# Lightning attention and a cosine-gated MLP on one core: a list scheduler's order, an enforced order of transfers, tiles of 4,2,4,4,4,4,2 blocks and other PSUM banks at both ends

## The chip, the cores and the metric

One core of one Trainium2 chip runs the kernel. The metric is the device time of one launch in microseconds (us). The kernel before took 254.38 us as the median of three runs (253.71 to 255.58). The engines are TensorE (PE in the profile, PEld for its weight loads), VectorE (DVE), ScalarE (ACT), GpSimd (POOL) and SyncE (SP); the last two also issue the transfers here.

## The reference, cut to what matters

Batch 4, 8 heads, 768 positions, head size 64; then a layer from 512 to 2048 and back to 512 features for the 3072 tokens.

```
for b in range(nb):                       # blocks of 64 positions, state carried
    intra = (qb @ kb.T) * Dmask           # lam ** (i - j), causal
    out[b] = intra @ vb + (qb * lam_pow) @ kv_state
    kv_state = lam_block * kv_state + (kb * rev_pow).T @ vb
x = out.transpose(0, 2, 1, 3).reshape(B * S, H * D)
h = x @ w_in
g = h * np.cos(h)
return (g @ w_out).astype(np.float32)
```

## The kernel before, in words

The kernel works on blocks of 128 positions of one batch, 24 blocks in all, 6 for each batch. The decay is taken out of the mask: queries are scaled by lam to the power of the position, values by its inverse, and the mask only cuts the triangle.

**Attention of a block n.** SP loads q, k and v (256 KB each, line 57, four buffers of each). POOL scales q and casts it (`q_s`, line 117), casts k (`k_b`, 119) and scales v into the zero-padded `v_pad` (122, three buffers). PE transposes q and k, 8 small matmuls into the PSUM bank `ps_t` (129); DVE copies that to `qkT` (134) and spreads the queries over the block-diagonal `q_bd` (137, two instructions). PE makes the scores in two halves (144), DVE masks each half (`s_m`, 151), PE makes the state update `ps_kv` (179, not for the last block of a batch) which DVE copies to `kv_bd` (191, two instructions), and PE makes the values `ps_o` (159 and 162), which ACT casts into the column block of `xT` (173).

**The layer.** A tile is 4 blocks, 512 columns, so there are 6 tiles. For each of 16 slices f of the hidden layer PE makes `ps_h` (4 matmuls of 512 columns, 199, two banks), ACT the cosine (205, as a sine with bias pi/2) and DVE the product `g` (212). Then, for each of the tile's 4 blocks, 16 matmuls of 512 columns in four groups of 4 make `ps_f` (219, one bank); ACT copies it out (226) and SP stores it (227).

**The order is written by hand.** The loop at the end of the kernel goes over i = -1, 0, ... and 16 slots s. Slot s of pass i holds slice s of the hidden layer of tile i, one of the four pieces of the attention of block 4(i+1) + s//4 (`attend`), and one group of four projection matmuls of tile i-1. Pass -1 is attention alone (the first 4 blocks), pass 0 has no projection, the last pass has projection alone. Each engine executes its instructions in the order in which they are written. The weights are cast on the way by transfers that POOL issues, 4 for `w_in` (103) and 4 for `w_out` (107), 512 KB each as they land; they stand between the preparations of blocks in POOL's queue, while SP runs ahead with the loads of further blocks.

Of the kernel before, what the change touches and what calls it, by code (L numbers as in the profile page):

```python
# [12 lines left out]
ALU = mybir.AluOpType  # L13


@with_exitstack
def kernel(
# [20 lines left out]
    T = 512  # L38
    NT = T // P
    NTILE = B * S // T  # L40

    ctx.enter_context(tc.manual_schedule())
    consts = ctx.enter_context(tc.tile_pool(name="consts", bufs=1))
    loads = ctx.enter_context(tc.tile_pool(name="loads", bufs=4))
    toks = ctx.enter_context(tc.tile_pool(name="toks", bufs=3))
    work = ctx.enter_context(tc.tile_pool(name="work", bufs=2))
    ps_1 = ctx.enter_context(tc.tile_pool(name="ps_1", bufs=1, space=bass.MemoryType.PSUM))
    ps_2 = ctx.enter_context(tc.tile_pool(name="ps_2", bufs=2, space=bass.MemoryType.PSUM))


    qf, kf, vf = {}, {}, {}

    def load(n):
        b, s0 = n // NB, (n % NB) * P
        for name, src, kept in (("q_f", q, qf), ("k_f", k, kf), ("v_f", v, vf)):
            t = loads.tile([P, H, D], F32, tag=name, name=name)
            nc.sync.dma_start(out=t, in_=src[b, :, s0:s0 + P, :].transpose([1, 0, 2]))  # L57
            kept[n] = t
# [3 lines left out]
    for n in range(3):  # L62
        load(n)


    lnl = consts.tile([P, H], F32)
    nc.scalar.activation(lnl, lam_bc, AF.Ln)
    pos = consts.tile([P, NB], F32)
    nc.gpsimd.iota(pos, pattern=[[P, NB]], base=0, channel_multiplier=1,
                   allow_small_or_imprecise_dtypes=True)  # L70
    expo = consts.tile([P, NB, H], F32)
    nc.vector.tensor_mul(expo, pos.unsqueeze(2).to_broadcast([P, NB, H]),
                         lnl.unsqueeze(1).to_broadcast([P, NB, H]))
    q_scale = consts.tile([P, NB, H], F32)
    nc.scalar.activation(q_scale, expo, AF.Exp)
    v_scale = consts.tile([P, NB, H], F32)
    nc.scalar.activation(v_scale, expo, AF.Exp, scale=-1.0)

# [8 lines left out]

# [4 lines left out]
    for t in v_pad + q_bd + kv_bd:  # L92
        nc.vector.memset(t, 0.0)

# [5 lines left out]

    def load_w_in(i):
        f0, f1 = i * D_FF // WCH, (i + 1) * D_FF // WCH
        nc.gpsimd.dma_start(out=w_in_sb[:, :, f0:f1], in_=w_in_src[:, :, f0:f1])

    def load_w_out(i):
        f0, f1 = i * KF // WCH, (i + 1) * KF // WCH
        nc.gpsimd.dma_start(out=w_out_sb[:, f0:f1, :], in_=w_out_src[:, f0:f1, :])


    q_s, k_b, qkT, s_m, xT = {}, {}, {}, {}, {}  # L110
    tr, sc, o_ps = {}, {}, {}
    kv_ps = ps_1.tile([P, NP, P], F32, tag="ps_kv", name="ps_kv")

    def prepare(n):
        c = n % NB
        q_s[n] = toks.tile([P, H, D], BF16, tag="q_s", name="q_s")
        nc.gpsimd.tensor_mul(q_s[n], qf.pop(n), q_scale[:, c, :].unsqueeze(2).to_broadcast([P, H, D]))  # L117
        k_b[n] = toks.tile([P, H, D], BF16, tag="k_b", name="k_b")
        nc.gpsimd.tensor_copy(k_b[n], kf.pop(n))  # L119
        v_n = vf.pop(n)  # L120
        for i in range(2):
            nc.gpsimd.tensor_mul(v_pad[n % NV][:, i::2, i * D:(i + 1) * D], v_n[:, i::2, :],  # L122
                                 v_scale[:, c, i::2].unsqueeze(2).to_broadcast([P, NP, D]))

    def transposes(n):
        t = ps_1.tile([P, 2, NP, P], BF16, tag="ps_t", name="ps_t")
        for i, src in enumerate((q_s.pop(n), k_b[n])):
            for p in range(NP):
                nc.tensor.transpose(t[:, i, p, :], src[:, 2 * p:2 * p + 2, :], ident)  # L129
        tr[n] = t  # L130

    def transposes_out(n):
        t = toks.tile([P, 2, NP, P], BF16, tag="qkT", name="qkT")
        nc.vector.tensor_copy(t, tr.pop(n))  # L134
        for i in range(2):
            h = slice(i * D, (i + 1) * D)
            nc.vector.tensor_copy(q_bd[n % NQ][h, :, i, :], t[h, 0, :, :])  # L137
        qkT[n] = t

    def scores(n, half):  # L140
        t = ps_2.tile([P, 4, P], F32, tag=f"ps_s{half}", bufs=1, name=f"ps_s{half}")
        for i in range(2):
            p = 2 * half + i
            nc.tensor.matmul(t[:, 2 * i:2 * i + 2, :], lhsT=qkT[n][:, 1, p, :],  # L144
                             rhs=q_bd[n % NQ][:, p, :, :], start=True, stop=True)
        sc[n, half] = t

    def scores_out(n, half):
        if half == 0:
            s_m[n] = toks.tile([P, H, P], BF16, tag="s_m", name="s_m")  # L150
        nc.vector.tensor_mul(s_m[n][:, 4 * half:4 * half + 4, :], sc.pop((n, half)),  # L151
                             mask.unsqueeze(1).to_broadcast([P, 4, P]))

    def values(n):
        c = n % NB
        t = ps_1.tile([P, NP, P], F32, tag="ps_o", name="ps_o")
        for p in range(NP):
            if c:
                nc.tensor.matmul(t[:, p, :], lhsT=kv_bd[(n - 1) % NK][:, p, :],  # L159
                                 rhs=qkT[n][:, 0, p, :], start=True, stop=False)  # L160
            for i in range(2):
                nc.tensor.matmul(t[:, p, :], lhsT=v_pad[n % NV][:, 2 * p + i, :],  # L162
                                 rhs=s_m[n][:, 2 * p + i, :],
                                 start=(i == 0 and c == 0), stop=(i == 1))
        o_ps[n] = t
        s_m.pop(n)
        qkT.pop(n)

    def values_out(n):
        i, j = n // NT, n % NT  # L170
        if j == 0:
            xT[i] = work.tile([P, KD, T], BF16, tag="xT", name="xT")
        nc.scalar.copy(xT[i][:, :, j * P:(j + 1) * P], o_ps.pop(n))  # L173

    def update(n):
        c = n % NB
        for p in range(NP):
            v_n = v_pad[n % NV][:, 2 * p:2 * p + 2, :].rearrange("p h e -> p (h e)")
            nc.tensor.matmul(kv_ps[:, p, :], lhsT=k_b[n][:, 2 * p:2 * p + 2, :],  # L179
                             rhs=v_both(n, p), start=(c == 0 and p == 0), stop=True,  # L180
                             skip_group_check=True)
        k_b.pop(n)

    def v_both(n, p):
        t = v_pad[n % NV][:, 2 * p, :]
        return bass.AP(tensor=t.tensor, offset=t.offset, ap=[list(t.ap[0]), [P + D, 2], [1, D]])

    def update_out(n):
        for i in range(2):
            h = slice(i * D, (i + 1) * D)  # L190
            nc.vector.tensor_copy(kv_bd[n % NK][h, :, h], kv_ps[h, :, h])  # L191


    g, hid, f_out = {}, {}, {}

    def ffn_in(i, f):
        t = ps_2.tile([P, T], F32, tag="ps_h", name="ps_h")
        for kd in range(KD):
            nc.tensor.matmul(t, lhsT=w_in_sb[:, kd, f * P:(f + 1) * P], rhs=xT[i][:, kd, :],  # L199
# [32 lines left out]
    def begin(n):  # L232
        if n + AHEAD + 1 < NBLK:
            load(n + AHEAD + 1)
        if n + AHEAD < NBLK:
            prepare(n + AHEAD)

# [73 lines left out]
```

## Time and profile before

| | us |
|---|---|
| median of three runs | 254.38 |
| the profiled execution | 252.93 |
| its span, first to last instruction | 251.2 |
| PE busy / DVE busy / ACT busy / POOL busy | 218.3 / 146.4 / 98.1 / 75.5 |

The span is what the rows are read from. Start times count from the first instruction. A matmul's own duration includes its way through the array; in the chain of waits it is shown by its spacing, so four matmuls of 512 columns there are 0.86 us at the full clock. A row of a DMA under an engine's queue (SPq, POOL) is the issuing, not the transfer.

### The profile page before, as it was taken

The numbers are of one execution on the slowest core, as the hardware profiler recorded it, in microseconds if no ns is written. First come the engines' busy times: TensorE is split into PE (matmuls) and PEld (weight loads), VectorE is DVE, ScalarE is ACT, GpSimd is POOL, SyncE is SP. The second block draws the span as 40 slices with busy tenths as digits, with TensorE's granted clock in tenths as the row PEclk, the third lists the DMA queues.
The fourth block names the chain that finished last, engine by engine and source line by source line (L and its number), as shares of the span: only waits on it lengthen the run. The fifth ranks groups of instructions, "written<-read, shape, count | busy, mean of one in ns | idle before, by whom it ended". The sixth has DMA issues, their size and how long they took to land.

```text
span 251.2 us, 3773 instructions
## 1 busy us (share of the span) xinstructions
PE 218.3 (87%) x1408; PEld 120.4 (48%) x1408; DVE 146.4 (58%) x265; ACT 98.1 (39%) x150; POOL 75.5 (30%) x113
## 2 busy tenths in 40 slices
PE   0555677868799999999999999999999999998873
PEld 0344544434455555555555555555555544443331
DVE  3877737797568655866775676668667534333000
ACT  5000045535353445345435544443454354543110
POOL 3885643655413324214421433242100000000000
PEclk9999779999999999999999999999999999999999
DMA  6999999999506735753674377347110111111111
GB/s 133 218 216 223 229 189 224 197 225 221 103 24 146 166 79 93 167 128 91 117 168 115 76 148 167 88 82 168 43 44 0 42 44 42 42 42 42 44 76 49
DMA packets 82722, 29.61 MB, mean 118 GB/s; under 512 B 75536, under 2 KB 79632, under 8 KB 82704
## 3 DMA queue, kind: packets, MB, share of 16 engines
q1 hardware_dynamic: 78480, 25.18, 46.8%
q0 software_dynamic: 4224, 4.19, 10.6%
q8 instruction: 11, 0.18, 0.3%
q14 instruction: 7, 0.06, 0.1%
HBM read 27.27 MB, written 6.29 MB: 134 GB/s over the span
## 4 chain that ended last, share of the span: by engine, by line
PE 78%; DVE 13%; ACT 3%; DMA 2%; SPq 1%; issue 1%; POOL 0%; ACTq 0%
PE ps_f L219 33%; PE ps_h L199 30%; PE ps_o L162 4%; PE ps_t L129 4%; DVE s_m L151 4%; PE ps_s L144 3%; DVE g L212 3%; DVE q_bd L137 3%; DVE kv_bd L191 2%; DMA k_f<-in_k_dram 2%; DVE qkT L134 2%; PE ps_o L159 1%; PE ps_kv L179 1%; SPq L57 1%; ACT o_sb L226 1%; ACT cos_h L205 1%
## 5 line engine op out<-in xcount | busy, mean ns | idle before, releaser
L212 DVE TENSOR_TENSOR g<-ps_h,cos_h 128x512 bf16<-128x512 f32 x96 | 66.4, 691 | 72.4 <-ACT cos_h L205 70.7
L205 ACT ACTIVATE cos_h<-ps_h,halfpi 128x512 f32<-128x512 f32 x96 | 66.0, 687 | 97.1 <-PE ps_h L199 97.1
L199 PE MATMUL ps_h<-xT,w_in_sb 128*128 128x512 bf16 x384 | 99.8, 383 | 3.7 <-DVE g L212 2.4
L219 PE MATMUL ps_f<-w_out_sb,g 128*128 128x512 bf16 x384 | 96.6, 379 | 2.8 <-ACT o_sb L226 2.8
L199 PEld LDWEIGHTS <-w_in_sb 128*128 128x128 bf16 x384 | 37.4, 99 | 46.8 <-issue 5.7
L219 PEld LDWEIGHTS <-g 128*128 128x128 bf16 x384 | 35.7, 98 | 34.3 <-issue 3.9
L117 POOL TENSOR_TENSOR q_s<-q_f,q_scale 128x512 bf16<-128x512 f32 x24 | 25.1, 1046 | 61.0 <-DMA q_f<-in_q_dram 57.5
L122 POOL TENSOR_TENSOR v_pad<-v_f,v_scale 128x256 bf16<-128x256 f32 x48 | 28.8, 621 | 29.3 <-PE ps_o L162 18.5
L151 DVE TENSOR_TENSOR s_m<-ps_s,mask 128x512 bf16<-128x512 f32 x48 | 32.7, 682 | 0.2
L162 PE MATMUL ps_o<-s_m,v_pad 128*128 128x128 bf16 x192 | 20.3, 227 | 13.8 <-DVE s_m L151 13.8
L173 ACT CAST xT<-ps_o 128x512 bf16<-128x512 f32 x24 | 14.1, 585 | 30.2 <-PE ps_o L162 30.2
L162 PEld LDWEIGHTS <-v_pad 128*128 128x128 bf16 x192 | 15.7, 102 | 18.6 <-issue 15.6
L226 ACT COPY o_sb<-ps_f 128x512 f32<-128x512 f32 x24 | 14.1, 586 | 20.0 <-PE ps_f L219 20.0
L144 PE MATMUL ps_s<-q_bd,qkT 128*128 128x256 bf16 x96 | 20.1, 294 | 0.0
L134 DVE COPY qkT<-ps_t 128x1024 bf16<-128x1024 bf16 x24 | 16.4, 682 | 5.7 <-PE ps_t L129 5.7
L137 DVE COPY q_bd<-qkT 64x512 bf16<-64x512 bf16 x48 | 18.0, 376 | 1.2
L129 PE MATMUL ps_t<-ident,q_s 128*128 128x128 bf16 x96 | 10.7, 242 | 8.4 <-POOL q_s L117 8.4
L119 POOL CAST k_b<-k_f 128x512 bf16<-128x512 f32 x24 | 14.7, 611 | 10.7 <-DMA k_f<-in_k_dram 7.7
L191 DVE CAST kv_bd<-ps_kv 64x256 bf16<-64x256 f32 x40 | 16.7, 416 | 0.3
L159 PE MATMUL ps_o<-qkT,kv_bd 128*128 128x128 bf16 x80 | 15.5, 226 | 0.0
L129 PEld LDWEIGHTS <-q_s 128*128 128x128 bf16 x96 | 8.1, 109 | 13.5 <-POOL q_s L117 8.7
L144 PEld LDWEIGHTS <-qkT 128*128 128x128 bf16 x96 | 9.8, 106 | 9.5 <-issue 0.2
(27 smaller groups left out, 57.5 us busy)
## 6 DMA issues: line engine op xcount, KB each, us to landing
q_f<-in_q_dram SPq DMA_DIRECT2D x24, 256.0 KB, 4.1
k_f<-in_k_dram SPq DMA_DIRECT2D x24, 256.0 KB, 4.6
v_f<-in_v_dram SPq DMA_DIRECT2D x24, 256.0 KB, 5.1
out_dram<-o_sb SPq DMA_DIRECT2D x24, 256.0 KB, 2.2
w_in_sb<-in_moe_w_in_dram POOLq DMA_DIRECT2D x4, 512.0 KB, 7.4
w_out_sb<-in_moe_w_out_dram POOLq DMA_DIRECT2D x4, 512.0 KB, 7.9
lam_bc<-in_lam_dram SPq DMA_DIRECT2D x1, 4.0 KB, 2.8
```

The lines of the kernel that those rows point to most:

```text
L117: nc.gpsimd.tensor_mul(q_s[n], qf.pop(n), q_scale[:, c, :].unsqueeze(2).to_broadcast([P, H, D]))
L122: nc.gpsimd.tensor_mul(v_pad[n % NV][:, i::2, i * D:(i + 1) * D], v_n[:, i::2, :], v_scale[:, c, i::2].unsqueeze(2).to_broadcast([P, NP, D]))
L129: nc.tensor.transpose(t[:, i, p, :], src[:, 2 * p:2 * p + 2, :], ident)
L137: nc.vector.tensor_copy(q_bd[n % NQ][h, :, i, :], t[h, 0, :, :])
L144: nc.tensor.matmul(t[:, 2 * i:2 * i + 2, :], lhsT=qkT[n][:, 1, p, :], rhs=q_bd[n % NQ][:, p, :, :], start=True, stop=True)
L151: nc.vector.tensor_mul(s_m[n][:, 4 * half:4 * half + 4, :], sc.pop((n, half)), mask.unsqueeze(1).to_broadcast([P, 4, P]))
L162: nc.tensor.matmul(t[:, p, :], lhsT=v_pad[n % NV][:, 2 * p + i, :], rhs=s_m[n][:, 2 * p + i, :], start=(i == 0 and c == 0), stop=(i == 1))
L191: nc.vector.tensor_copy(kv_bd[n % NK][h, :, h], kv_ps[h, :, h])
L199: nc.tensor.matmul(t, lhsT=w_in_sb[:, kd, f * P:(f + 1) * P], rhs=xT[i][:, kd, :], start=(kd == 0), stop=(kd == KD - 1))
L205: nc.scalar.activation(c, hid[i, f], AF.Sin, bias=halfpi)
L212: nc.vector.tensor_mul(g[i][:, f, :], h, c)
L219: nc.tensor.matmul(f_out[i], lhsT=g[i][:, f, j * P:(j + 1) * P], rhs=w_out_sb[:, f, :], start=(f == 0), stop=(f == KF - 1))
```

## The change: what it does

1. **A planner sets the order.** Every piece of work becomes a task with an engine, a written duration, what it depends on and a priority; a list scheduler walks through time, always starts the task that can start first and, among those that can start together on an engine, the one of lowest priority number. The instructions are then written out in the order of planned starts. The priority of the attention of a tile is the planned time of the layer one tile earlier, less 4 us.
2. **Transfers in enforced order.** `ORDER` lists 4 blocks, 4 chunks of w_in, 4 of w_out; the rest of the blocks follow. Where the kind changes, an added dependency makes the first transfer behind the change wait until the next to last one ahead of it has landed.
3. **Tiles** have 4, 2, 4, 4, 4, 4 and 2 blocks; the matmuls of the hidden layer have 128 columns per block of the tile, so 128 of the 448 have 256.
4. **Banks.** The scores share one pair of banks `ps_s`. In tile 0 every third slice of the hidden layer uses the bank `ps_f`; in the last tile the two projections use `ps_f` and `ps_s`.
5. **The first 4 blocks** are prepared on three engines: q on DVE, k on ACT, v on POOL. The DVE's zero fills come before the scale factors, the ACT table of the sine is loaded by a one-element instruction at the start, and positions count from the middle.
6. The output tile `o_sb` has three buffers.

```
+TILES = [4, 2, 4, 4, 4, 4, 2]
+ORDER = "b0 b1 b2 b3 i0 i1 i2 i3 o0 o1 o2 o3"
...
+            for eng, c in first.items():
+                t0 = min(a for a, _ in c)
+                a, t = min(((a, t) for a, t in c if a <= t0 + 1e-6), key=lambda x: x[1].prio)
+                if best is None or a < best[0]:
+                    best = (a, t)
...
+    BUFS = {"ld": 4, "tok": 3, "ps_t": 1, "ps_s": 2, "ps_o": 1, "ps_h": 2, "ps_f": 1, "cos": 2, "o_sb": 3}
...
+    warm = consts.tile([P, 1], F32)
+    nc.scalar.activation(warm, halfpi, AF.Sin)
...
+    unit = [MM(n * P, 4 * KF) + MM(DM, KF * n) + 1.78 * n for n in TILES]
+    begins = [sum(unit[:i]) for i in range(len(unit) + 1)]
+    def prio_attn(n, part):
+        i = next(i for i in range(len(TILES)) if n < first[i + 1])
+        if i == 0:
+            return -1000.0 + n + part
+        return begins[i - 1] + unit[i - 1] * (n - first[i] + part) / TILES[i] - 4.0
...
+        a = pl.add("DVE" if early else "POOL", 0.69 if early else 1.05, [load_t["q_f", n]], prep_q, pa(-0.9), get="q_s")
+        b = pl.add("ACT" if early else "POOL", 0.61, [load_t["k_f", n]], prep_k, pa(-0.9), get="k_b")
+        d = pl.add("POOL", 1.2, [load_t["v_f", n], V.get(n - NV), U.get(n - NV)], prep_v, pa(-0.9))
...
+            tag = "ps_f" if i == 0 and f % 3 == 2 else "ps_h"
+            h = pl.add("PE", MM(cols, 4), [Vo[n] for n in range(n0, n0 + nb)] + [w_t["in", f * WCH // KF]],
+                       hidden, pr, get=tag)
...
+            tag = ("ps_f", "ps_s", "ps_o", "ps_s")[j % 4] if i == len(TILES) - 1 else "ps_f"
...
+        deps = [kept[-2]] if at and (names[at - 1][0] == "b") != (which == "b") else []
...
+    for t in pl.order():
+        if t.emit:
+            t.ins = t.emit()
```

POOL's queue at the start, from the second block's preparation on. Before: the preparations of whole blocks, with a weight transfer after each from the third on.

```order
L117 TENSOR_TENSOR q_s<-q_f,q_scale 128x512
L119 CAST k_b<-k_f 128x512
L122 TENSOR_TENSOR v_pad_116<-v_f,v_scale 128x4x64 x2
L117 TENSOR_TENSOR q_s<-q_f,q_scale 128x512
L119 CAST k_b<-k_f 128x512
L122 TENSOR_TENSOR v_pad_117<-v_f,v_scale 128x4x64 x2
L103 DMA w_in_sb<-in_moe_w_in_dram 128x4x512
L117 TENSOR_TENSOR q_s<-q_f,q_scale 128x512
L119 CAST k_b<-k_f 128x512
L122 TENSOR_TENSOR v_pad_115<-v_f,v_scale 128x4x64 x2
L103 DMA w_in_sb<-in_moe_w_in_dram 128x4x512
```

And in the changed kernel, from the second block's values on:

```order
L249 TENSOR_TENSOR v_pad_87<-v_f,v_scale 128x4x64 x2
L249 TENSOR_TENSOR v_pad_88<-v_f,v_scale 128x4x64 x2
L213 DMA w_in_sb<-in_moe_w_in_dram 128x4x512 x2
L249 TENSOR_TENSOR v_pad_86<-v_f,v_scale 128x4x64 x2
L213 DMA w_in_sb<-in_moe_w_in_dram 128x4x512 x2
L216 DMA w_out_sb<-in_moe_w_out_dram 128x4x512 x4
L234 TENSOR_TENSOR q_s<-q_f,q_scale 128x512
L243 CAST k_b<-k_f 128x512
L249 TENSOR_TENSOR v_pad_87<-v_f,v_scale 128x4x64 x2
```

All 8 weight transfers now stand before the preparation of block 4; q and k of the first blocks have left this queue.

SP's queue in the changed kernel at the border between the loads of block 3 and of block 4, with what each waits for (DMAHW and DMASW are landings of SP's and of POOL's transfers, the other names engines that free the buffer):

```order
L198 DMA q_f<-in_q_dram 128x8x64 [waits DMAHW2_49]
L198 DMA k_f<-in_k_dram 128x8x64 [waits DMAHW3_49]
L198 DMA v_f<-in_v_dram 128x8x64 [waits DMAHW4_49]
L198 DMA q_f<-in_q_dram 128x8x64 [waits DMAHW5_49,DMASW6_49,DVE_49]
L198 DMA k_f<-in_k_dram 128x8x64 [waits DMAHW6_49,Activation_49]
L198 DMA v_f<-in_v_dram 128x8x64 [waits DMAHW7_49,Pool_49]
```

The fourth row is block 4's q: it now waits for POOL's seventh transfer (the third chunk of w_out), which it did not before, and everything behind it in the queue waits with it.

DVE in the changed kernel, from the end of block 5's attention into the hidden layer of tile 1 (two blocks, so 256 columns), and the attention of blocks 6 and 7 (before, four products of 512 columns stood beside the attention of one block):

```order
L269 COPY qkT<-ps_t 128x1024
L276 COPY q_bd_89<-qkT 64x4x128 x2
L315 CAST kv_bd_91<-ps_kv 64x4x64 x2
L375 TENSOR_TENSOR g<-ps_h,cos 128x256
L296 TENSOR_TENSOR s_m<-ps_s,mask 128x512 x2
L269 COPY qkT<-ps_t 128x1024
L276 COPY q_bd_90<-qkT 64x4x128 x2
L375 TENSOR_TENSOR g<-ps_h,cos 128x256
L315 CAST kv_bd_92<-ps_kv 64x4x64 x2
L296 TENSOR_TENSOR s_m<-ps_s,mask 128x512 x2
```

Between the start of the projection of tile 0 and the hidden layer of tile 2, DVE now has the attention of seven blocks and 16 products of 256 columns.

## Rows read from the trace of the kernel before

**Rows 1.** The page's first part: busy time, share, instructions of each engine.

```profile
PE 218.3 (87%) x1408; PEld 120.4 (48%) x1408; DVE 146.4 (58%) x265; ACT 98.1 (39%) x150; POOL 75.5 (30%) x113
```

**Rows 2.** Windows: stretch, length, busy time (instructions) by engine, clock, DMA share, GB/s.

```profile
32.00:38.00 6.00, 4.94 (x28) 2.76 (x28) 2.21 (x5) 3.01 (x4) 2.29 (x3) 0.72 1.16 181
44.00:62.00 18.00, 13.80 (x104) 7.95 (x103) 14.82 (x28) 8.18 (x13) 10.35 (x15) 1.00 1.20 215
98.00:130.00 32.00, 32.00 (x221) 17.79 (x219) 21.22 (x40) 14.61 (x23) 9.99 (x15) 1.00 0.56 125
```

**Rows 3.** Chain of waits, first 37 us: start, duration, what.

```profile
16.16 0.87 PE ps_t L129 x8
...
21.95 0.87 PE ps_t L129 x8
...
33.50 1.81 PE ps_h L199 x4
...
36.17 1.36 PE ps_h L199 x4
```

**Rows 4.** Groups by line: busy us, mean ns of one, idle before and its releaser.

```profile
L212 DVE TENSOR_TENSOR g<-ps_h,cos_h 128x512 bf16<-128x512 f32 x96 | 66.4, 691 | 72.4 <-ACT cos_h L205 70.7
L205 ACT ACTIVATE cos_h<-ps_h,halfpi 128x512 f32<-128x512 f32 x96 | 66.0, 687 | 97.1 <-PE ps_h L199 97.1
L151 DVE TENSOR_TENSOR s_m<-ps_s,mask 128x512 bf16<-128x512 f32 x48 | 32.7, 682 | 0.2
L173 ACT CAST xT<-ps_o 128x512 bf16<-128x512 f32 x24 | 14.1, 585 | 30.2 <-PE ps_o L162 30.2
L134 DVE COPY qkT<-ps_t 128x1024 bf16<-128x1024 bf16 x24 | 16.4, 682 | 5.7 <-PE ps_t L129 5.7
L191 DVE CAST kv_bd<-ps_kv 64x256 bf16<-64x256 f32 x40 | 16.7, 416 | 0.3
```

**Rows 5.** Timeline of the first 8 us: the first block's preparation on ACT, POOL, DVE.

```profile
3.89 1.28 ACT L75 ACT_TABLE_LOAD   x1
...
5.33 0.23 ACT L77 ACTIVATE v_scale<-expo 128x48 f32<-128x48 f32 x1
...
6.49 0.61 POOL L119 CAST k_b<-k_f 128x512 bf16<-128x512 f32 x1
...
7.81 0.69 DVE L134 COPY qkT<-ps_t 128x1024 bf16<-128x1024 bf16 x1 [0.36 <-PE ps_t L129]
```

**Rows 6.** The copies into q_bd between 5 and 34 us: duration ns min/median/max.

```profile
L137 DVE COPY q_bd<-qkT x10: 291/651/1130, 8.5 to 29.8; 64x512 bf16<-64x512 bf16 x10
```

**Rows 7.** The same copies between 98 and 194 us.

```profile
L137 DVE COPY q_bd<-qkT x22: 284/288/292, 102.2 to 188.9; 64x512 bf16<-64x512 bf16 x22
```

**Rows 8.** SP's queue: the issue of block 3's k.

```profile
11.72 1.14 SPq L57 DMA_DIRECT2D k_f<-in_k_dram  x1
```

**Rows 9.** The page's sixth part: KB of each transfer, median us to landing.

```profile
k_f<-in_k_dram SPq DMA_DIRECT2D x24, 256.0 KB, 4.6
...
w_in_sb<-in_moe_w_in_dram POOLq DMA_DIRECT2D x4, 512.0 KB, 7.4
```

**Rows 10.** The tile w_in_sb: time to landing of its four transfers.

```profile
DMA to landing us min/median/max: 6.0/7.4/8.4
```

**Rows 11.** Windows, one short stretch: length, clock, DMA share, GB/s.

```profile
20.60:21.60 1.00, 1.00 1.26 209
```

**Rows 12.** Chain of waits in the middle: one block's worth of slots, first and last.

```profile
106.96 0.86 PE ps_f L219 x4
...
115.64 0.86 PE ps_f L219 x4
```

**Rows 13.** Chain of waits at the end, and the last copy.

```profile
230.62 3.63 PE ps_f L219 x16
...
234.90 3.63 PE ps_f L219 x16
...
247.26 0.59 ACT o_sb L226
```

More of the change, by code (lines that the diff above doesn't have):

```diff
@@ L46 @@
+    toks = ctx.enter_context(tc.tile_pool(name="toks", bufs=BUFS["tok"]))
     work = ctx.enter_context(tc.tile_pool(name="work", bufs=2))
[L47 to L58, printed above, removed]
+    psum = ctx.enter_context(tc.tile_pool(name="psum", bufs=1, space=bass.MemoryType.PSUM))
@@ L70 @@
                    allow_small_or_imprecise_dtypes=True)
[L71 to L77, printed above, removed]
     ident = consts.tile([P, P], BF16)
@@ L99 @@
     WCH = 4
[L101 to L114, printed above, removed]
-        c = n % NB
[L116 to L160, printed above, removed]
-            for i in range(2):
[L162 to L199, printed above, removed]
-                             start=(kd == 0), stop=(kd == KD - 1))
-        hid[i, f] = t
@@ L258 @@
[L258 to L280 removed]
+    kv_ps = psum.tile([P, NP, P], F32, tag="ps_kv", name="ps_kv")
@@ new lines, with add_w, emit @@
+    w_t = {}
+    def add_w(which, c, prio, deps=()):
+        def emit():
+            if which == "in":
+                a, z = c * D_FF // WCH, (c + 1) * D_FF // WCH
+                i = nc.gpsimd.dma_start(out=w_in_sb[:, :, a:z], in_=w_in_src[:, :, a:z])
+            else:
+                a, z = c * KF // WCH, (c + 1) * KF // WCH
+                i = nc.gpsimd.dma_start(out=w_out_sb[:, a:z, :], in_=w_out_src[:, a:z, :])
+            for d in deps:
+                tc.add_manual_dep(i.ins, getattr(d, "issue", d).ins.ins.name, mybir.DependencyInfo(
+                    mybir.DependencyClass.Sync, mybir.DependencyReason.DATA), reason="order of loads")
+            return i
+        _, w_t[which, c] = dma("POOL", 2.6, 0.9, emit, prio, deps)
@@ new lines @@
+    add = {}
+    names = ORDER.split()
+    names += [f"b{n}" for n in range(NBLK) if f"b{n}" not in names]
+    kept = []
+    for at, name in enumerate(names):
+        which, n = name[0], int(name[1:])
+        deps = [kept[-2]] if at and (names[at - 1][0] == "b") != (which == "b") else []
+        if which == "b":
+            add_load(n, at, deps)
+            kept += [load_t[x, n] for x in ("q_f", "k_f", "v_f")]
+        else:
+            add_w({"i": "in", "o": "out"}[which], n, at, deps or ([hold] if hold else []))
+            kept.append(w_t[{"i": "in", "o": "out"}[which], n])
+        hold = deps[0] if deps else (None if which == "b" else hold)
@@ L284 @@
+    for i in range(len(TILES)):
+        for n in range(first[i], first[i + 1]):
+            add_attention(n)
+        add_ffn(i)
+    for t in pl.order():
+        if t.emit:
+            t.ins = t.emit()
 _INS = ['q', 'k', 'v', 'lam', 'moe_w_in', 'moe_w_out']
```

331 lines of the change are left out of this document (253 added, 78 removed).

## The prediction

> **What bounds the kernel now.** I read the page first: PE is busy 87% of the span, DVE 58% [rows 1], so PE is the bound on the whole, but not everywhere. The windows tell where: between 98 and 130 us PE is busy 32.00 of 32 us, between 44 and 62 us only 13.80 of 18, while DVE has 14.82 there [rows 2]. The chain of waits gives the three stages. Until 33.50 us there is attention alone, in a cycle of 5.8 us per block (21.95 less 16.16), though PE has little to do in it [rows 3]: it goes DVE, PE, DVE. Then tile 0's hidden layer shares DVE with the attention of tile 1, past 62 us. From 98 us at the latest to 230 us PE alone is the chain. Last comes the projection of the last tile: each group of 16 matmuls waits for the copy of the one before, 0.65 us (230.62 and 3.63 to 234.90), four times [rows 13].
>
> **PE's own work.** In the full stage a block costs 8.68 us from 106.96 to 115.64 [rows 12]: eight groups of four matmuls at 0.863, so 1.78 for its attention. For 24 blocks that is 208.3. Four blocks that end a batch have no update, and three that begin one (beside the first) no old state: by their columns about 0.2 each, 1.5 together. So from the first hidden slice on, with four blocks' attention behind it (7.1), PE has 208.3 - 7.1 - 1.5 = **199.7 us** to do, in either kernel. Narrower tiles change the number of matmuls and not the columns. Before, it took from 33.50 to 247.2: 14 us are idle or slow. The change can gain there and in the 33.5 us ahead.
>
> **The start.** The loads of the first four blocks stand in SP's queue as before. The sine's table moves ahead of k's first cast: v_scale ends at 5.56, the table takes 1.28 [rows 5], a one-element instruction at most 0.23 (v_scale's row), the cast on ACT 0.59 (the xT cast of [rows 4]): 7.64, where POOL's cast ended at 7.10 [rows 5]. So the first qkT moves from 7.81 to **8.35**. From there DVE is the chain: per block qkT 0.68, two masks 1.36, kv_bd 0.83 [rows 4] and the pair of q_bd copies. That pair is the open price: 2 x 0.288 undisturbed [rows 7], 2 x 0.651 in this stage, where POOL was busy most of the time [rows 6]. I take 0.80, nearer the lower, because POOL keeps only v here. That makes 3.67 a block, 14.7 for four. Three of the four q scalings now lie in this chain; DVE's product of 512 columns is 0.68 [rows 4], so 2.0. They cover the way over PE and back that DVE waited for. 8.35 + 14.7 + 2.0, some 0.5 for handovers, 0.4 for the last values and 0.6 for the xT copy: the first hidden slice starts at **26.7** instead of 33.5 (25.8 with the lower pair, 28.7 with the upper).
>
> **The weights.** Block 3's k is issued at 11.72 [rows 8] and lands 4.6 later [rows 9], at 16.3. That releases the first chunk. The nearest price for it is the fastest landing, 6.0 [rows 10]: 22.3. The next follow at the rate of the stretch from 20.6 us, 209 GB/s [rows 11], 2.5 us per 512 KB: w_in is there at 29.8, needed at 37; the seventh chunk, which releases block 4's q, at 37.4; the eighth at 39.9, needed at 45. So tile 0 waits for no weight. POOL's fourth v stands between the chunks and waits for the first block's values, done long before.
>
> **Tile 0.** 16 slices of 0.863 are 13.8 us. With three banks in turn a slice's product (0.86 + 0.69 + 0.69 [rows 4] and handovers, 2.45) is done before its bank is wanted again, 2.59 later; that it is so near is a risk of some tenths. The clock: before, the first two slices took 1.81 and 1.36 [rows 3], in a window with a granted clock of 0.72, a mean of full (2.4 GHz) and half [rows 2]; over 0.86 each that is 1.45 too much. PE comes out of the same thin stage, where it had long waits, so I keep **1.45** (0 if the clock is up by then). The hidden layer ends at 42.0. The first projection needs ps_f back from slice 14: **0.7** more. It starts at 42.7, and block 4's transposes stand behind it at 46.2. Its k was released at 37.4, is issued some 1.2 later, lands at 43.3 and is cast by 43.9 (0.61 [rows 5]). The cover is 2.3 us; if the weights are later than that, the rest is paid one for one.
>
> **Projection of tile 0 to hidden layer of tile 2.** In this stretch PE has 32.0 us (16 groups at 0.863, 16 half slices at 0.43, the attention of six blocks and part of a seventh). DVE has 8 qkT, 7 pairs of q_bd, 14 masks, 6 kv pairs and 16 products of 256 columns. The half product is not in the trace: below it lies the kv copy of 256 columns, 0.42, above it the full product, 0.69 [rows 4]; I take 0.45, because the columns are the same as in the former. Sum: 5.4 + 5.6 + 9.5 + 5.0 + 7.2 = 32.7. With both engines full and passing work to and fro, DVE decides; with some 1.8 of its own waits it takes 34.5, so PE loses **2.5** (0.5 if it hardly waits; 6 with the upper pair).
>
> **Tiles 2 to 5.** In the order two projection groups, a slice and the update, 2.8 us, stand between a block's transposes and its scores. DVE needs qkT 0.68, a product 0.69, the pair 0.8 and handovers, 2.4, and may be inside another product when the transposes end. Before, this margin held in every slot. I take **2.0** for some 12 blocks, between 0 and 5. The banks: where a projection follows another, a full slice or two half slices (0.86) cover the copy, 0.65; nothing.
>
> **The end.** The last two projections have banks of their own, so the 0.65 per block is gone. Behind PE's last matmul stays what stood there: from 247.2 (0.07 ahead of the copy at 247.26 [rows 13]) to the end of the span, 4.0.
>
> **Sum.** 26.7 + 199.7 + 1.45 + 0.7 + 2.5 + 2.0 + 4.0 = 237.1 us of span, against 251.2. The profiled execution took 1.7 more than its span, 238.8, and the median of the runs 1.45 more than that: **240 us**, 14 less than 254.38.
>
> **A rule that speaks against a part of it.** The rows show that q_bd's copies, 0.288 alone, took up to 1.130 beside POOL's work [rows 6, 7]. The Trainium skill, page "SBUF — State Buffer", section "Who interferes with whom", says more: a DVE instruction with two SBUF inputs shuts out a GpSimd instruction that reads SBUF, and the other way round, for a whole instruction. By that rule the moved q scaling too would wait for POOL's v; the sum would be about 242. No run here shows q's scaling on DVE; for the copies the trace agrees.
>
> **The rivals.**
> (a) *POOL holds DVE up throughout.* If the pair costs 1.30 wherever POOL works, as it did on the median in the first stage [rows 6], the start is 2.0 longer, the stretch to tile 2 3.5 longer, and in tiles 2 to 5 DVE's 2.9 is over the 2.8 that PE leaves, with some 0.3 to 0.4 for each block more than I took, 4: together 9.5, **250 us**. For it: the planner counts on 0.6, and what it orders has no slack for more. Against: POOL does less in the first stage, and from 98 us on the pair was undisturbed in all 11 blocks [rows 7], though POOL did the same work per block. The page named above would have it this way wherever the two meet. Chance 0.12.
> (b) *Block 4 waits behind the weights, and it gets slower.* If the chunks go one after the other at the 7.4 us from issue to landing that they took [rows 9], the seventh lands at 16.3 + 7 x 7.4 = 68, block 4's k is cast at 74.5, and PE, which executes in order, stands before its transposes 28 us longer: **266** or so with the waits that this one swallows. It begins to cost when the seventh lands after 39.7 and has used up the gain at about 54. Against: those 7.4 us were shared with SP's loads, and none of POOL's transfers waits for another. Chance 0.05.
> (c) *Nothing is in the way.* Lower pair, full clock at tile 0, DVE's waits hidden, nothing in tiles 2 to 5: 240 - 0.9 - 1.45 - 2 - 2, **234 us**. For it: the durations written into the planner are those of the rows, and before PE had no idle time at all from 98 to 130 us [rows 2]. Chance 0.13.
> That the order is not enforced is no case: the queues name the landings for which they wait.
>
> **Numbers.** The forecast, 237 to 245, has 0.70. The range 234 to 248 leaves out (b), most of (a) and a little of (c), about 0.17. One per cent is 2.5 us, what a measurement here can tell from none; (b) alone can come near or over the old time, so faster 0.95, same 0.01, slower 0.04.
>
> **What would show it.** The first hidden slice between 25.8 and 28.7 us; weights landing 2.5 us apart, the first at about 22; no wait of PE for POOL's q or k of block 4; block 4's transposes at about 46; PE idle of 2 to 6 us between there and tile 2, released by DVE (s_m, q_bd or g), not by transfers; no pause of 0.65 among the last two projections. I am wrong if PE's waits name POOL or a transfer after 40 us, if q_bd copies take over 0.6 on the median after tile 1, or if the hidden layer of tile 0 is spaced wider than 0.9 at the full clock.

## The result, and the profile after

The changed kernel took **238.2 us** (median of 4 runs, 237.34 to 239.19), the kernel before 254.98 on the same occasions (253.71 to 255.68): a ratio of 0.935 with a 95% interval of 0.929 to 0.941. The forecast was 240, with a range of 234 to 248. A later set gave 237.43 (236.47 to 237.76) and 0.932 (0.928 to 0.936). Some runs, of the kernel before above all, are slower, mostly at a lower granted clock; every ratio here leaves them out, a median keeps them. The profiled execution took 238.56 us, its span 236.8, where the sum had 238.8 and 237.1.

The page's first part, beside [rows 1]: PE is busy for about as long (215.4 us for 218.3), in a span that is 14.4 shorter; DVE has 6.4 more to do.

```profile
PE 215.4 (91%) x1447; PEld 123.9 (52%) x1472; DVE 152.8 (65%) x285; ACT 103.7 (44%) x171; POOL 68.6 (29%) x105
```

The chain of waits (start, duration, what) from the first block to the projection of tile 0, beside [rows 3, 5], and at the end, beside [rows 13]:

```profile
8.34 0.70 DVE qkT L269
...
26.32 0.59 PE ps_h L362
27.13 2.76 PE ps_h L362 x6
...
41.34 0.70 ACT cos L369
42.06 0.70 DVE g L375
42.81 3.63 PE ps_f L400 x16
...
225.91 0.86 PE ps_s L400 x4
226.78 3.45 PE ps_f L400 x16
230.23 2.60 PE ps_s L400 x12
...
232.85 0.59 ACT o_sb L413
```

The first hidden slice starts at 26.32 instead of 33.50 us, half of what the span lost. At the end 16 matmuls take 3.45 with nothing between the groups, where [rows 13] had 3.63 and a copy. The timeline of PE shows block 4's transposes at the place that the sum gave them, and the start of tile 2:

```profile
46.26 0.39 PE L264 MATMUL ps_t<-ident,q_s 128*128 128x128 bf16 x4
...
81.33 1.89 PE L362 MATMUL ps_h<-xT,w_in_sb 128*128 128x512 bf16 x7
```

Windows, with the columns of [rows 2] (the last three: granted clock, DMA share, GB/s), for the last part of the start, the first slices of tile 0, the rest of its hidden layer, the stretch to tile 2, and the middle:

```profile
19.90:26.30 6.40, 4.41 (x33) 3.31 (x31) 4.80 (x10) 1.17 (x2) 4.89 (x7) 0.50 1.24 206
26.30:30.20 3.90, 3.65 (x9) 1.36 (x10) 0.69 (x1) 0.95 (x2) 0.00 (x0) 0.51 1.24 202
30.20:42.00 11.80, 11.75 (x55) 5.33 (x55) 8.99 (x13) 9.32 (x14) 0.00 (x0) 1.00 1.18 199
46.50:81.50 35.00, 33.24 (x315) 23.75 (x318) 30.80 (x62) 13.04 (x26) 24.31 (x35) 1.00 1.15 230
112.00:200.00 88.00, 87.42 (x568) 47.84 (x578) 55.47 (x101) 40.60 (x63) 16.99 (x24) 1.00 0.18 55
```

The granted clock was at half, 1.2 GHz, until about 30.2 us, so three slices took 4.46 us (26.32 to 30.78) and not 2.59. The copies into q_bd (min, median and max in ns), in the first stage, the stretch to tile 2 and the middle, beside [rows 6, 7]:

```profile
L276 DVE COPY q_bd<-qkT x8: 284/288/548, 9.1 to 22.3; 64x512 bf16<-64x512 bf16 x8
...
L276 DVE COPY q_bd<-qkT x14: 284/572/1178, 47.6 to 77.8; 64x512 bf16<-64x512 bf16 x14
...
L276 DVE COPY q_bd<-qkT x18: 274/290/409, 113.8 to 190.0; 64x512 bf16<-64x512 bf16 x18
```

What PE waited for between 46 and 112 us, the whole list (total, times, longest):

```profile
PE ps_s L289 <- DVE q_bd L276: 1.1, 4, 0.3
PE ps_h L362 <- DVE g L375: 0.7, 2, 0.3
PE ps_f L400 <- ACT o_sb L413: 0.2, 1, 0.2
```

No transfer and no POOL among them. Block 4's q was issued at 39.02 us, after SP had waited for the weights since 14.1, and POOL took it up at once when it landed (timeline of SP and of POOL):

```profile
39.02 0.37 SPq L198 DMA_DIRECT2D q_f<-in_q_dram  x1
```

```profile
43.10 1.04 POOL L234 TENSOR_TENSOR q_s<-q_f,q_scale 128x512 bf16<-128x512 f32 x1 [18.31 <-DMA q_f<-in_q_dram]
```

### The profile page after: what moved, and what is told of

Read it like the earlier page. It is cut to its first block, busy times and chain, and to the rows that moved or that the text cites. A ratio compares the mean times of both kernels' runs of the same rounds, so it can differ in the third digit from the quotient of the medians.

```text
span 236.8 us, 3931 instructions
## 1 busy us (share of the span) xinstructions
PE 215.4 (91%) x1447; PEld 123.9 (52%) x1472; DVE 152.8 (65%) x285; ACT 103.7 (44%) x171; POOL 68.6 (29%) x105
## 4 chain that ended last, share of the span: by engine, by line
PE 77%; DVE 16%; ACT 3%; issue 1%; DMA 1%
PE ps_h L362 30%; PE ps_f L400 30%; DVE q_bd L276 5%; PE ps_o L331 4%; PE ps_t L264 4%; PE ps_s L289 3%; DVE qkT L269 3%; DVE s_m L296 3%; DVE g L375 2%; PE ps_f L362 2%; DVE kv_bd L315 2%; PE ps_o L328 2%; PE ps_s L400 1%; DMA lam_bc<-in_lam_dram 1%; DVE q_s L234 1%
## 5 line engine op out<-in xcount | busy, mean ns | idle before, releaser
L369 ACT ACTIVATE cos<-ps_h,halfpi 128x512 f32<-128x512 f32 (+1 forms) x107 | 66.3, 624 | 75.8 <-PE ps_h L362 73.6
L375 DVE TENSOR_TENSOR g<-ps_h,cos 128x512 bf16<-128x512 f32 (+1 forms) x107 | 64.5, 610 | 51.5 <-ACT cos L369 50.3
L362 PE MATMUL ps_h<-xT,w_in_sb 128*128 128x512 bf16 (+1 forms) x413 | 92.8, 350 | 2.3 <-ACT xT L340 0.7
L400 PE MATMUL ps_f<-w_out_sb,g 128*128 128x512 bf16 x358 | 91.1, 379 | 1.4 <-DVE g L375 0.6
L362 PEld LDWEIGHTS <-w_in_sb 128*128 128x128 bf16 x448 | 43.4, 99 | 38.9 <-issue 4.4
L296 DVE TENSOR_TENSOR s_m<-ps_s,mask 128x512 bf16<-128x512 f32 x48 | 31.3, 683 | 1.7 <-PE ps_s L289 1.4
L234 POOL TENSOR_TENSOR q_s<-q_f,q_scale 128x512 bf16<-128x512 f32 x20 | 20.9, 1046 | 29.3 <-DMA q_f<-in_q_dram 20.1
L276 DVE COPY q_bd<-qkT 64x512 bf16<-64x512 bf16 x48 | 19.8, 413 | 0.7
L289 PE MATMUL ps_s<-q_bd,qkT 128*128 128x256 bf16 x96 | 16.3, 285 | 4.4 <-DVE q_bd L276 4.3
L243 POOL CAST k_b<-k_f 128x512 bf16<-128x512 f32 x20 | 12.3, 615 | 7.1 <-issue 5.6
```

What stands on the lines that cost most here:

```text
L234: eng.tensor_mul(t, live.pop(("q_f", n)), q_scale[:, c, :].unsqueeze(2).to_broadcast([P, H, D]))
L289: nc.tensor.matmul(t[:, 2 * i:2 * i + 2, :], lhsT=live["qkT", n][:, 1, p, :], rhs=q_bd[n % NQ][:, p, :, :], start=True, stop=True)
L296: nc.vector.tensor_mul(live["s_m", n][:, 4 * half:4 * half + 4, :], live.pop(("s", n, half)), mask.unsqueeze(1).to_broadcast([P, 4, P]))
L362: ins = nc.tensor.matmul(t[:, :cols], lhsT=w_in_sb[:, kd, f * P:(f + 1) * P], rhs=live["xT", i][:, kd, :cols], start=(kd == 0), stop=(kd = ...
L369: nc.scalar.activation(c[:, :cols], live["h", i, f][:, :cols], AF.Sin, bias=halfpi)
L375: nc.vector.tensor_mul(live["g", i][:, f, :cols], live.pop(("h", i, f))[:, :cols], live.pop(("c", i, f))[:, :cols])
```

## The experiments

Twelve runs, eleven other kernels and the changed one again, in three sets; each set has its runs of the kernel before on the same chip, but the changed kernel itself stands only in the third. Ratios are to the kernel before; differences in us to the changed kernel are between sets, beside the 0.8 us by which its own two medians differ. Four questions: whether the start was won by the order or by splitting the preparation; what the enforced order of transfers is worth; what the tiles and the banks are worth; and who takes what PE still loses after tile 0. The places that they are read from:

| kernel | first slice | first projection | block 4's transposes | tile 2 | PE's end | span |
|---|---|---|---|---|---|---|
| changed | 26.32 | 42.81 | 46.26 | 81.33 | 232.83 | 236.8 |
| changed, again | 25.86 | 41.97 | 45.42 | 79.46 | 231.50 | 235.5 |
| no added waits | 27.31 | 44.42 | 48.91 | 84.99 | 236.49 | 240.5 |
| q and k on POOL | 24.84 | 41.14 | 47.15 | 81.58 | 233.57 | 237.5 |
| q_bd on ACT | 25.97 | 41.88 | 45.33 | 79.18 | 229.18 | 233.2 |
| unread matmuls | 25.68 | 41.06 | 44.52 | 79.47 | 231.37 | 235.4 |
| both: POOL, ACT | 25.09 | 42.24 | 48.25 | 81.87 | 231.63 | 235.6 |
| those and matmuls | 24.85 | 39.46 | 45.92 | 79.64 | 229.39 | 233.4 |

(start times in us, from each kernel's timeline of PE and its chain of waits; the profiled execution of each. The first two rows are one kernel: they tell how far one execution is from the next.)

### The order of transfers without its waits

```
-            for d in deps:          # at the loads, and at the weights
+            for d in ():
```

> The changed kernel with the same instructions in the same order on every engine, but without the added waits between kinds of transfers: block 4's loads no longer wait for the third chunk of w_out, nor w_in for block 3's k. Theory (the enforced order is what keeps the weights on time): SP then issues the loads of blocks 4 to 7, 3 MB, from about 13 us on, and the weights share the DMA engines with them; at the 200 to 220 GB/s that both together get, some 15 us of foreign traffic stand ahead of the last weights, so w_out is complete at about 50 us instead of 39, and PE, which wants its last chunk at 45.4, stands 3 to 8 us: 241 to 246 us. Rival (the weights have slack of that size, and the order alone is what gained): 237 to 239 us, with the first projection still at about 43 us.

Measured 241.66 us (241.45 to 242.19), ratio 0.947 (0.938 to 0.956): 3.5 us more than the change, the low end of the theory's range. PE at tile 0's projection:

```profile
44.42 2.75 PE L400 MATMUL ps_f<-w_out_sb,g 128*128 128x512 bf16 x12 [0.64 <-DVE g L375]
48.05 1.02 PE L400 MATMUL ps_f<-w_out_sb,g 128*128 128x512 bf16 x4 [0.88 <-DMA w_out_sb<-in_moe_w_out_dram]
```

The wait for w_out is there, but it is only 0.88 us. The table shows the rest, beside its first row: 1.0 is lost before the first slice, 0.6 in tile 0's hidden layer, 1.0 between block 4's transposes and tile 2. So the theory's way, one long wait for w_out, makes up a quarter of its number. And what ran ahead was no use: block 5's k was issued 23 us earlier than in the changed kernel, its issue alone took 9.33 us, and POOL cast it at 46.05 instead of 47.83 us.

```profile
19.31 9.33 SPq L198 DMA_DIRECT2D k_f<-in_k_dram  x1
```

### The preparation: put back on POOL, and split in the kernel before

```
-        early = n < TILES[0]
+        early = False
```

> The changed kernel with q and k of the first four blocks prepared on POOL again, as before the change; DVE loses four q scalings of 0.69 us, POOL gets 4 x 1.66 us more to do. Theory (the start was won by the order of the instructions, in which DVE never waits for the way over PE and back): the first hidden slice starts at 26 to 28 us (26.3 with the preparation split), as what DVE saves it pays in stretched q_bd copies; 237.5 to 240 us. Rival (the start was won by taking the preparation off POOL): the cycle of 5.8 us per block comes back, the first hidden slice starts at 30 to 33 us, 242 to 245 us.

Measured 237.78 us (237.16 to 239.28), 0.933 (0.925 to 0.941): no difference. The start is *earlier*, beyond what the theory had: 24.84 us. The q_bd copies there are slower, as expected:

```profile
L276 DVE COPY q_bd<-qkT x8: 284/506/1041, 8.4 to 21.1; 64x512 bf16<-64x512 bf16 x8
```

Their eight sum to 4.46 us against 2.66 in the changed kernel. But DVE is rid of three q scalings in its chain (0.67, 0.69 and 0.99 us), and the first qkT comes 0.6 earlier, since k's cast no longer waits on ACT for the sine's table. By tile 2 the lead is gone (81.58 for 81.33); where it went is the question of the combinations. The reverse, in the kernel before:

```
-        nc.gpsimd.tensor_mul(q_s[n], ...)
+        (nc.vector if n < NT else nc.gpsimd).tensor_mul(q_s[n], ...)
-        nc.gpsimd.tensor_copy(k_b[n], kf.pop(n))
+        (nc.scalar.copy if n < NT else nc.gpsimd.tensor_copy)(k_b[n], kf.pop(n))
+    nc.scalar.activation(warm, halfpi, AF.Sin)      # ahead of the loop
```

> The kernel before with one part of the change alone: q of the first four blocks scaled by DVE, k cast by ACT, the sine's table loaded ahead; the order written by hand stays. Theory (the cycle of 5.8 us per block at the start comes from the order, in which DVE waits for PE and PE for DVE in turn, not from POOL's preparation): what the q_bd copies win beside a quieter POOL, 0.7 us a block, DVE pays for q; the first hidden slice stays at 32 to 34.5 us, the ratio within 0.99 to 1.01. Rival (the preparation on POOL made the start long): the first slice 4 to 7 us earlier, a ratio of 0.972 to 0.985.

Measured 256.28 us beside 255.59, ratio 1.003 (0.997 to 1.008). The chain:

```profile
34.21 0.58 PE ps_h L202
```

So it was not the split that won the start: in the old order it gave nothing, and in the new one it cost 1.0 to 1.5 us. What is left is the planner's order, with the enforced transfers in it, whose waits are worth about 1.0 there (27.31 without them). The parts of the order were not tried one by one.

### The end alone, in the kernel before

```
-            f_out[i] = ps_1.tile([P, DM], F32, tag="ps_f", name="ps_f")
+            tag = "ps_f" if i < NTILE - 1 or j % 2 == 0 else "ps_t"
+            f_out[i] = ps_1.tile([P, DM], F32, tag=tag, name=tag)
```

> The kernel before with one part of the change alone: in the last pass the projections of the four blocks use two banks in turn. Theory (each of the four groups of 16 matmuls waits 0.65 us for the copy of the one before): the four pauses go, 2.0 to 2.6 us less than before, a ratio of 0.990 to 0.992. Rival (the weight loads or the first use of another bank cost as much): no difference.

Measured 252.79 us beside 255.59, ratio 0.989 (0.984 to 0.994). In its chain the groups stand close. One of the four pauses is left, before the first of them, so the rows account for 2.0 us of the 1.4 to 4.0 that the interval allows:

```profile
240.07 3.45 PE ps_f L220 x16
243.53 3.47 PE ps_t L220 x16
```

### Banks and tiles undone

```
-            t = bank("ps_f" if i == 0 and f % 3 == 2 else "ps_h", [P, 4 * P], F32)
+            t = bank("ps_h", [P, 4 * P], F32)
-            tag = ("ps_f", "ps_s", "ps_o", "ps_s")[j % 4] if i == len(TILES) - 1 else "ps_f"
+            tag = "ps_f"
```

> The changed kernel without the added PSUM banks at both ends: the hidden layer of tile 0 on its two banks alone, the projections of the last tile on one. Theory (a slice holds its bank for 2.45 us, product of PE, cosine and product of DVE with handovers, so two banks give a slice every 1.23 us instead of every 0.86): the hidden layer of tile 0 takes 5.8 us longer, the first projection's wait of 0.6 is gone, the end gets two pauses of 0.65; 243 to 245 us. Rival (the third bank only covers handovers, and what is lost in tile 0 is won back because block 4's data are there in time): 239 to 240.5 us.

Measured 242.7 us (241.82 to 243.02), 0.953 (0.947 to 0.959): 4.5 more, just under the theory's range. PE's timeline in tile 0, with two banks:

```profile
33.06 1.98 PE L362 MATMUL ps_h<-xT,w_in_sb 128*128 128x512 bf16 x8 [0.55 <-DVE g L375]
35.59 1.76 PE L362 MATMUL ps_h<-xT,w_in_sb 128*128 128x512 bf16 x7 [0.55 <-DVE g L375]
```

Two slices every 2.53 us: a slice's bank is free again 2.53 us after its start, where I had worked out 2.45. With three banks in turn, 2.59 us, that leaves less than 0.1, and it was enough: in the changed kernel no slice of tile 0 waited for DVE.

The 4.5 us are not the theory's sum, though. With ps_f free the planner put the first projections between the slices, from 37.40 on, and tile 2 began at 83.33, 2.0 later than in the changed kernel and not 5.8: most of what tile 0 lost was won back, as the rival said, if not by its way. The other 2.4 came behind tile 2, 1.3 of it as two pauses at the end. From the chain:

```profile
37.56 0.86 PE ps_f L400 x4
...
229.34 3.63 PE ps_f L400 x16
232.99 0.59 ACT o_sb L413
233.62 3.63 PE ps_f L400 x16
```

```
-TILES = [4, 2, 4, 4, 4, 4, 2]
+TILES = [4, 4, 4, 4, 4, 4]
```

> The changed kernel with six tiles of four blocks instead of 4,2,4,4,4,4,2; the planner sets the order anew. Theory (the tile of two blocks packs the attention of seven blocks and 16 products of 256 columns into one stretch, where DVE is the bound, which cost PE 3.2 us): with four blocks in tile 1 the stretch has 2.7 us of DVE's work per 3.5 us of PE's, the loss there falls to about 1, and 236 to 237.5 us come out. Rival (the small tiles are needed, the first so that the hidden layer of tile 1 comes early, the last for a short end): 239 to 241 us.

Measured 239.06 us (237.76 to 240.17), 0.940 (0.933 to 0.948): within the scatter of the changed kernel, so neither is borne out. PE's waits from 40 us to 120 us were 3.1 us here and 2.6 there. What the small tiles are worth is less than can be told here.

### q_bd on ACT

```
-                nc.vector.tensor_copy(q_bd[n % NQ][h, :, i, :], t[h, 0, :, :])
+                (nc.vector.tensor_copy if early else nc.scalar.copy)(q_bd[n % NQ][h, :, i, :], t[h, 0, :, :])
```

(and the planner's duration, 1.2 us on ACT)

> The changed kernel with the q_bd copies from block 4 on made by ACT instead of DVE. Theory (between the projection of tile 0 and tile 2 DVE is the bound, and what makes it so are these copies, 0.57 us on the median there and up to 1.18 beside POOL's work, against 0.29 alone): the 3.2 us that PE loses between 46.5 and 81.5 us fall under 1, and the 1.7 lost after it too: 234.5 to 236.5 us. Rival (in that stretch the way from transposes over the copies to the scores is what PE waits for, whichever engine copies, and ACT is slower at it and busy with cosines): no gain or a loss, 238 to 241 us, PE's waits now naming ACT's q_bd.

Measured **235.85 us** (234.89 to 236.06), 0.924 (0.916 to 0.931). Window, copies and waits of PE from 46 to 232 us:

```profile
46.50:81.50 35.00, 34.95 (x335) 25.43 (x333) 26.30 (x53) 22.88 (x44) 24.73 (x36) 1.00 1.06 226
```

```profile
L276 ACT COPY q_bd<-qkT x16: 604/615/620, 46.7 to 77.1; 64x512 bf16<-64x512 bf16 x16
```

```profile
PE ps_f L400 <- ACT o_sb L413: 0.2, 1, 0.2
```

From block 4 to its end PE is hardly ever short of work any more, though a copy costs ACT more than twice what it costs an undisturbed DVE. It is also the same every time, beside the same work on POOL (24.7 us against 24.3) that stretched DVE's to 1178 ns. From block 4's transposes to PE's end it takes 183.85 us, the changed kernel 186.57 (186.08 in its second profile): 2.7 less (2.2), of which the list of PE's waits above shows 1.8; the rest lies in pauses that it doesn't name. The stretch to tile 2 took 33.85 here against 35.07, what lies behind it 150.0 against 151.5. This order has one block's scores more ahead of tile 2 (32 score matmuls for 28, 0.43 us), so 1.65 were won in the stretch and 1.1 behind it. In the second profile of the changed kernel the q_bd copies of the stretch took 290 ns on the median (max 1040) and not 572, the stretch 34.04, and most of the gain, 1.6 of 2.2, lies behind it. So how far the copies are drawn out differs between executions of one kernel, and PE waits for DVE either way (second profile, 24 to 240 us):

```profile
PE ps_h L362 <- DVE g L375: 1.0, 3, 0.3
...
PE ps_s L289 <- DVE q_bd L276: 0.7, 1, 0.7
```

Moving the copies takes both their spread and their plain time off DVE, 30.8 us of work in the first profile's window against 26.3 here; which of the two counts for more is not shown. The 3.2 of the expectation was too much: it rested on my count of 32.0 us of PE's work up to tile 2. This run, with PE full, puts it at 33.6, and at 33.2 for the changed kernel's order, which leaves about 1.9. The Trainium skill, page "SBUF — State Buffer", section "Who interferes with whom", gives ScalarE ports of its own and only DVE and GpSimd a shared pair: the trace agrees, with 604 to 620 ns on ACT and 284 to 1178 on DVE.

### Matmuls that nobody reads

```
+            for _ in range(2):                  # into a free bank, after U[1], U[2], U[3] and V[3]
+                nc.tensor.matmul(t, lhsT=ident, rhs=zero, start=True, stop=True)
```

> The changed kernel with eight matmuls of 512 columns that nobody reads added on PE, two after each state update of the second to the fourth block and two after the fourth block's values, in the places where PE waited 0.4 to 1.2 us. Theory (the clock was at half, 1.2 GHz, from 19.9 to 30.15 us because PE waited 1.2 and 0.4 us for DVE just before, and about 2 us were lost by it): the granted clock stays at full over the start, the first slices of the hidden layer take 0.86 us each instead of 1.7, and the whole takes 236 to 237 us. Rival (the clock falls whatever PE does there, or the added matmuls stand in front of what DVE waits for): clock at half as before or later start of the first slice, 238 to 239.5 us.

Measured 237.1 us (236.03 to 237.13), 0.928 (0.921 to 0.936): 1.1 less than the change in its first set, but 0.3 less than in its last, so by the times alone not shown. The windows are clearer, if not clean: a granted clock of 0.82 from 20 to 26 us and 0.95 from 26 to 40, where the changed kernel had 0.50 and 0.85 in one profile and 0.96 and 0.90 in the other. The first two slices took 2.48 us here (1.73 at the full clock), so the first was still slow, and the expectation's "stays at full" was not met.

In this run PE also stood 0.26 us for POOL's k of block 4, at 45.16:

```profile
45.16 0.40 PE L266 MATMUL ps_t<-ident,k_b 128*128 128x128 bf16 x4 [0.26 <-POOL k_b L245]
```

The windows:

```profile
20.00:26.00 6.00, 4.03 (x30) 2.37 (x28) 4.09 (x9) 1.17 (x2) 4.59 (x7) 0.82 1.24 207
26.00:40.00 14.00, 14.00 (x63) 6.20 (x62) 9.53 (x14) 10.02 (x15) 0.00 (x0) 0.95 1.24 202
```

### The combinations

> The changed kernel once more, on the same chip as the three combinations below, so that they can be held against it. Expected 237.3 to 239.2 us, as its runs so far; the first slice of the hidden layer at 26.3 us, the granted clock at half after it for some slices or not at all, which makes its scatter.

Measured 237.43 us, ratio 0.932 (0.928 to 0.936).

```
-        early = n < TILES[0]
+        early = False                # q, k of the first blocks on POOL
+        ...                          # and q_bd on ACT from block 4 on
```

> Two edits together: q and k of the first blocks on POOL again (the first slice of the hidden layer then came at 24.8 us, 1.5 earlier, but the time hardly moved) and the q_bd copies from block 4 on by ACT (235.85 us alone). Theory (the 1.5 us won at the start were lost again in the stretch up to tile 2, where DVE was the bound): with DVE relieved there they come through, 234 to 235 us, 1 to 1.5 less than with ACT's copies alone. Rival (what holds the early start back is block 4, whose q and k are on POOL at 43 to 45 us in every version, because the enforced order ties them to the weights): 235.5 to 236.2 us, no gain over ACT's copies alone.

Measured 236.11 us (234.93 to 237.31), 0.927 (0.923 to 0.931): the rival's number. Its six runs differ as their mean granted clock does: 234.93 and 235.02 us at 1.00, 236.11 to 236.28 at 0.99, and 237.31, the profiled one of the table, at 0.984. With the unread matmuls besides:

> The same with the eight unread matmuls of 512 columns besides, which kept the clock at full at the start of tile 0. Theory: another 0.8 to 1.4 us less than the two edits together, 232.8 to 234 us, and less scatter. Rival (block 4's data): the first projection starts earlier but PE then waits for POOL's k of block 4 ahead of its transposes, 234 to 235.5 us, with that wait of 0.5 us or more in the trace.

Measured 235.38 us (235.09 to 235.9), 0.925 (0.922 to 0.929), the granted clock at full all the way in the profile and 0.997 to 1.00 in all six runs. Here the matmuls steadied the clock and added nothing beyond that: the two runs of the kernel without them that had the clock at 1.00 were no slower. The first projection starts at 39.46, 2.5 to 3.4 us earlier than in the changed kernel; PE's end is at 229.39, where ACT's copies alone had 229.18. All that was won ahead is gone by tile 2 (79.64 and 79.18). Who took it, from PE's waits and POOL's timeline:

```profile
PE ps_f L415 <- ACT o_sb L428: 0.7, 1, 0.7
PE ps_o L344 <- DVE s_m L298: 0.7, 1, 0.7
...
PE ps_h L377 <- DVE g L390: 0.4, 1, 0.4
PE ps_f L415 <- DMA w_out_sb<-in_moe_w_out_dram: 0.3, 1, 0.3
```

```profile
43.98 1.04 POOL L236 TENSOR_TENSOR q_s<-q_f,q_scale 128x512 bf16<-128x512 f32 x1 [18.91 <-DMA q_f<-in_q_dram]
```

POOL takes up block 4's q at 43.98; in every version with the enforced order that was between 42.8 and 44. The planner, which counts on that landing, fills the time ahead with 24 projection matmuls instead of 16, and these stand before w_out's last chunk and before the copy out of ps_f; the attention then comes late, and its waits with it. The rival named a wait for POOL's k; it took this form. Whether an earlier issue helps:

```
-        deps = [kept[-2]] if ...
+        deps = [kept[-3 if which == "b" else -2]] if ...
```

> The same as the run with the unread matmuls, but block 4's loads wait for the second chunk of w_out instead of the third; the orders on PE, DVE, ACT and POOL are the same. If block 4's data are what PE waits for in that run, they come 2 to 2.5 us earlier and up to 1 us is won, 232 to 233.5 us; the last chunks of w_out then land up to 2.5 us later, at about 42, just when they are wanted. If block 4 is no bound there, no difference, or a loss of up to 1 us where the last chunk comes late.

Measured 235.25 us (234.97 to 235.76), 0.924 (0.920 to 0.928): no difference. The issue came 2.7 us earlier (39.97 in the run above), POOL took the data up 0.2 earlier:

```profile
37.30 0.37 SPq L200 DMA_DIRECT2D q_f<-in_q_dram  x1
...
38.39 3.43 SPq L200 DMA_DIRECT2D v_f<-in_v_dram  x1
```

```profile
43.77 1.04 POOL L236 TENSOR_TENSOR q_s<-q_f,q_scale 128x512 bf16<-128x512 f32 x1 [18.75 <-DMA q_f<-in_q_dram]
```

From 20 to 40 us the DMA engines move 196 to 205 GB/s in this run and in every kernel of the table. Earlier release did not bring block 4's data in sooner beside the weights. Without the enforced order POOL had block 4's q at 24.73, and w_out was late instead; so what comes first can be chosen, and the whole was not there earlier in any version. That it is this rate which sets the limit fits these runs, but none changes the rate. So a start earlier than about 26 us brought nothing that can be told here, and the version to keep is the one edit, q_bd on ACT: its 0.924 and the 0.925 and 0.924 of the combinations can't be told apart. Not tried: the unread matmuls with ACT's copies alone, in the order that reaches block 4 after 16 projection matmuls.

## Why the prediction was right

- **The start**: 26.32 (and 25.86) for 26.7, the first qkT at 8.34 for 8.35. The chain was as worked out, DVE's, and its terms near: q_bd 2.66 us for four blocks (3.2 taken), q's scaling 2.35 (2.0). (The terms as listed add to 26.55, not 26.7.) One sentence of the step fell: that the scalings "cover the way over PE and back that DVE waited for". They lie in the chain themselves: with q and k on POOL the first slice comes 1.5 us earlier, 0.6 of it by the first qkT, and without the new order the split wins nothing.
- **The weights**: no wait, as said. Block 3's k let POOL issue the first chunk at 17.2 where I had 16.3, block 4's q was issued at 39.0 where I had 37.4, its k was cast by 44.9 for 43.9, its transposes stood at 46.26 for 46.2. So the cover was 1.3 us and not 2.3, and what other versions won ahead of it came to nothing.
- **Tile 0**: the clock took 1.87 us (1.45), the bank 0.64 (0.7), the third bank held with 0.1 us to spare.
- **After tile 0** is where sizes were off, in both directions. PE's own work from the first slice on was 199.7 by the sum; the run with ACT's copies takes 203.2 for it, less 1.3 for the clock (three slices in 3.88 us) and 0.87 of waits: 201.0. The 1.3 that the sum lacks lie nearly all ahead of tile 2, where I had counted 32.0 and the runs give 33.2. The two losses to DVE, 2.5 and 2.0, came to about 3.0: from 26.32 to 232.83 there are 206.5, less 201.0, the clock and the bank. Up to tile 2 that is about 1.9, just under the 2 to 6 named as a sign. Their cause was right: moving the copies off DVE brought 2.2 to 2.7 back. That the span came within 0.3 of the sum is in part luck, as 1.3 too little and 1.5 too much nearly cancel.
- **The end**: 4.0 for 4.0, and no pause between the last groups.
- **The rivals**: (a) DVE held up throughout did not come, though its condition was half there: the copies took 572 ns on the median up to tile 2, near the 0.6 beyond which I would have been wrong, but 290 there in the second profile, and 290 in the middle. The q scaling on DVE took 0.67 to 0.69 us three times and 0.99 once, from 18.26 on, while POOL issued two chunks of weights (until 18.89) and then began its v (18.90); which of these held it up is not shown. The sum by rows held (237.1; 236.8 measured), not the 242 by the Trainium skill's page "SBUF — State Buffer", section "Who interferes with whom": the trace agrees in so far as the one scaling that ran beside POOL's work was drawn out, but the two hardly met. (b) was to cost something once the seventh chunk lands after 39.7 us, and it landed at 39.0: 0.7 us away, but 15 from the point where the gain is gone, since the eight chunks shared the DMA engines and the last was in by 41.4 (issued at 24.0, 17.4 to landing).

Where the 14.4 us of span came from: 7.2 from the start; 2.6 from the four pauses at the end; the other 4.6 are what is left, in between, where in the kernel before PE was idle for 4.2 us from 44 to 62 us alone [rows 2]. That they come from attention and hidden layer no longer alternating slot by slot is argued; no run takes that part by itself. The enforced transfers (3.5) and the banks (4.5) are what these gains need, not gains beside them; the tiles and the split preparation gave nothing that can be measured.

## What to carry to other kernels

Before an early stage is made faster, look for the landing behind it: if the transfers bring in no more up to that point whatever their order (196 to 205 GB/s here), an earlier start only moves the wait, as it did here at 44 us. When an engine at 65% of the span holds up one at 91%, look at its copies whose duration varies from row to row, and try them on an engine where the duration is constant, even if it is twice as long. A planner's order carries its durations with it: most edits here also reordered PE, so the comparison must be made at fixed places of the work (first slice, first projection, block 4, tile 2, end), not by the total alone, and beside two executions of one kernel.

## What the runs showed of the hardware that was not expected

- The same copy of 64 x 512 bf16 inside SBUF: 284 to 1178 ns on DVE beside POOL, 604 to 620 on ACT beside the same. On DVE its median in one stretch was 572 ns in one execution and 290 in another of the same kernel.
- The issue of one load by SP took 0.37 to 1.3 us as a rule; beside the weights it took 9.33 with the four loads of blocks 4 and 5 issued ahead of it in a row, 6.92 and 6.42 for the two behind it, and 3.43 for block 4's v in the last run.
- The granted clock just ahead of tile 0 differs between executions of one kernel (0.50 and 0.96 from 20 to 26 us). With the eight unread matmuls and q and k on POOL it was 1.0, and the runs lie within 0.8 us (235.09 to 235.9) where the same kernel's without the matmuls lie within 2.4.
